# Attention and two dense layers on one core: staging tiles, thresholds on ScalarE, and keys of two heads turned in one go

## The chip, the cores and the metric

One core of a Trainium2 chip runs the kernel. The metric is the device time of one execution in microseconds; lower is better. Engines are named as in the profile: PE is TensorE, DVE is VectorE, ACT is ScalarE, POOL is GpSimd, SP is SyncE, which here only issues DMAs. PEld is the loading of PE's weights, which runs beside its matmuls.

## The reference

There are 4 batches of 8 heads, 576 positions and 64 dimensions a head, all in float32. The attention keeps only scores within tau of the row's maximum; its output is the input of two dense layers with 2048 hidden columns.

```python
scores = scale * np.matmul(q, k.transpose(0, 1, 3, 2))
thresh = np.max(scores, axis=-1, keepdims=True) - tau
scores = np.where(scores >= thresh, scores, -1000000000.0)
scores = scores - np.max(scores, axis=-1, keepdims=True)
attn = np.exp(scores)
attn = attn / (np.sum(attn, axis=-1, keepdims=True) + 1e-09)
x = np.matmul(attn, v)            # then (tokens, heads * dim)
h = x @ w_in;  x = np.where(h >= 1, h, np.where(h <= -1, 0, (h + 1) ** 2 / 4)) @ w_out
h = x @ w_in2; x = (h * np.clip(h + 3, 0, 6) / 6) @ w_out2
```

## The kernel before, in words

Float32 products are made from halves: a number is split into a high part, rounded to PE's fast float32 format (fp32r in the profile), and a low part, the remainder, and the products of the parts are added up in PSUM.

The attention runs over 16 jobs, each a batch and a pair of heads. A job has 9 blocks of 128 query rows: four of each head, and one (block 4) with the last 64 rows of both heads. A block (`em_block`) goes like this: PE makes the scores of 128 rows by 576 keys in a pair of PSUM banks (P0 or P1, in turn); DVE copies them out negated and keeps the row's minimum nm (L329); ACT makes the exponential e with nm as bias (L330); a threshold th = nm + tau is made for each row (L331), on POOL in the first four jobs and on DVE from the fifth on; DVE multiplies e with the mask p <= th and sums the row into z (L334). Three blocks later `em_pt` turns p by PE, and ACT and DVE copy it out of PSUM. In the first five jobs it goes straight into the tile Gf, and the product with the values runs as plain float32. From the sixth job on the copy goes into one of two staging tiles pf (L376, the tail L350 or L352), ACT writes the high part Gh from pf (L379), and POOL the low parts (L380, L381). `pv_chunk` multiplies with the values, a chunk at a time between other work of PE; from the sixth job on its two halves of 64 rows are added by way of a staging tile named fold (L420, L422). After the ninth block `pre_norm` adds 1e-9 to z (L429) and inverts it, and `em_norm` spreads the result over rows by PE, multiplies, and stores the job's output in DRAM.

Queries and keys come in before their job. `load_qk` loads one head's queries (twice side by side, in qn) or keys (kn, one tile for all). `pre_k` splits a head's keys into the tile ksp, on POOL but for the very first (L233, L234). `unit_qk` turns them by 5 transposes into a P bank and copies them out: the queries split by ACT and DVE (L270, L271), the keys as they are by ACT (L280). A job's four such units stand at its blocks 0, 1 and, for the next job, 5 and 6.

The weights of the dense layers arrive as raw 64-bit words and are put together by `split_a` and `split_b` over ACT, DVE and POOL. During the attention `split_a` clears the sign bit on DVE (L119) and clips on POOL (L121); afterwards ACT takes the absolute value (L124).

When the first batch has its four jobs, pieces of the first dense layer (`dense1`, lines L540 to L608) are woven in: after each third of an attention step a credit of 0.3484 is added, and pieces are emitted while it lasts. What is left comes after the attention, and then the rest of both layers (L540, L582).

The order of the text is the order of priority. A planner puts each engine's instructions in order when the kernel is built, by its own model of their durations, and sets the waits; each engine then works through its list in order. DMAs are all issued from SP's list, in order.

Of the kernel before, what the change touches and what calls it, by code (L numbers as in the profile page):

```python
# [18 lines left out]
def kernel(  # L19
# [12 lines left out]
    nc = tc.nc  # L32
# [20 lines left out]
    CSTEP = 2  # L53
    RAW = 3
# [12 lines left out]
    three = const.tile([128, 1], F32, name="three")  # L67

# [39 lines left out]
    def split_a(kind, m, f):  # L108
# [104 lines left out]
    def load_qk(j, nm, h):  # L213
# [3 lines left out]
        src = (q if nm == "q" else k)[b, 2 * hp + h]  # L217
        main = src[0:MAIN, :].rearrange("(p c) d -> p c d", c=4)
        if nm == "q":
            nc.sync.dma_start(out=qn[h][:, 0:4], in_=main.unsqueeze(2).to_broadcast([128, 4, 2, D]))  # L220
            nc.sync.dma_start(out=qn[h][64 * h:64 * h + TAIL, 4],
                              in_=src[MAIN:SEQ, :].unsqueeze(1).to_broadcast([TAIL, 2, D]))
        else:
            nc.sync.dma_start(out=kn[:, 0:4, :], in_=main)
            nc.sync.dma_start(out=kn[0:TAIL, 4, :], in_=src[MAIN:SEQ, :])

    def pre_k(j, h):
# [28 lines left out]
    def unit_qk(j, nm, h):  # L256
# [3 lines left out]
        if nm == "q":  # L260
            n = qn[h].rearrange("p c r d -> p c (r d)")
            for c in range(5):
                x = T.transpose(tm[:, c * 128:(c + 1) * 128], n[:, c, :], ident)
                if c == 0:
                    pe_pins.append(x)
            load_qk(j + 1, "q", h)
            hi, lo = qst[h]
            sc = taus[:, 1:2]
            tm = tm[:, 0:MAIN + 128]
            S.activation(out=hi, in_=tm, func=ACTF.Copy, scale=sc)  # L270
            V.scalar_tensor_tensor(out=lo, in0=tm, scalar=sc, in1=f32(hi), op0=ALU.mult, op1=ALU.subtract)  # L271
        else:
            n = f32(natt.pop(("ks", j, h))).rearrange("p c r d -> p c (r d)")
            for c in range(4):
                x = T.transpose(tm[:, c * 128:(c + 1) * 128], n[:, c, :], ident)
                if c == 0:
                    pe_pins.append(x)
            T.transpose(tm[:, MAIN:MAIN + 128], n[:, 4, :], ident)
            kst[j, h] = ap.tile([128, SEQ], F32R, tag=f"kst{h}", name="kst")
            S.activation(out=kst[j, h], in_=tm[:, 0:SEQ], func=ACTF.Copy)  # L280

# [26 lines left out]
    def em_block(j, i):  # L308
# [20 lines left out]
        V.tensor_scalar(out=p, in0=s, scalar1=-1.0, scalar2=3e38, op0=ALU.mult, op1=ALU.min, accum_out=nm)  # L329
        S.activation(out=e, in_=p, func=ACTF.Exp, bias=nm, scale=-1.0)  # L330
# [549 lines left out]
```

## Time and profile before

| | us |
|---|---|
| median of 3 runs | 1207.64 |
| lowest and highest | 1205.75, 1208.53 |
| the profiled execution, and its span | 1205.04, 1203.3 |
| PE busy | 1151.6 (96%) |
| PEld busy | 990.1 (82%) |
| POOL busy | 717.2 (60%) |
| ACT busy | 707.8 (59%) |
| DVE busy | 672.0 (56%) |

The attention's first score block is copied out at 9.9 us of the span, and its last at 499; the woven dense work starts at some 150 us. Busy shares over the whole span mix these parts with the dense layers, so they are read by stretch. PE's busy time counts the tails of pipelined matmuls.

### The profile page before, as it was taken

To read this page: it belongs to the slowest core of one execution; us is meant where nothing else is said; L and a number is where in the kernel's file an instruction comes from. 1 tells how busy PE (TensorE), PEld (TensorE's weight loads), DVE (VectorE), ACT (ScalarE), POOL (GpSimd) and SP (SyncE) were. 2 spreads that over 40 slices of the span, in tenths; PEclk is the share of its full clock that TensorE was granted. 3 is DMA by queue.
4 is the path that set the end of the run, shared out by engine and by line. 5 is a ranking of instruction groups with operands and counts; after the bars stand their busy time and mean duration, and the time that the engine had idled before them with its cause. 6 is when DMAs were issued, how large, how long until landed. Compare 5 with 4: busy or idle time off the path is not lost.

```text
span 1203.3 us, 19343 instructions
## 1 busy us (share of the span) xinstructions
PE 1151.6 (96%) x6820; PEld 990.1 (82%) x6820; DVE 672.0 (56%) x1433; ACT 707.8 (59%) x1332; POOL 717.2 (60%) x745
## 2 busy tenths in 40 slices
PE   7899999999998998979999999999999999999998
PEld 5666679988887998979888998888888888888886
DVE  6989997888878788765142465565641121121111
ACT  6777788888878788757354676655542222233222
POOL 5888679999988898947252566656742222222221
PEclk9999999999999999989999999999999999999999
DMA  6444431122221220134121244443210010010000
GB/s 162 129 126 129 137 111 45 43 73 56 55 78 52 55 77 22 35 109 129 62 70 36 88 136 141 160 152 113 88 31 27 1 57 10 1 45 1 18 1 36
DMA packets 99857, 87.08 MB, mean 72 GB/s; under 512 B 51376, under 2 KB 83632, under 8 KB 99760
## 3 DMA queue, kind: packets, MB, share of 16 engines
q1 hardware_dynamic: 99760, 85.85, 24.0%
q8 instruction: 54, 0.88, 0.3%
q14 instruction: 43, 0.35, 0.1%
HBM read 68.52 MB, written 17.30 MB: 71 GB/s over the span
## 4 chain that ended last, share of the span: by engine, by line
PE 70%; POOL 12%; DVE 8%; issue 4%; ACT 3%; DMA 2%; SPq 0%; POOLq 0%; DVEq 0%; ACTq 0%
PE Q L540 29%; PE P L582 26%; POOL Gl L380 6%; PE Q L597 4%; PE P L318 3%; PE Q L408 3%; POOL Gh L381 2%; DVE p L334 2%; PE Q L355 2%; PE Q L410 2%; DVE p L329 2%; POOL vst L294 1%; POOL gl L558 1%; POOL ksp L234 1%; DVE xl L524 1%
## 5 line engine op out<-in xcount | busy, mean ns | idle before, releaser
L558 POOL TENSOR_TENSOR gl<-r,gh 128x512 fp32r<-128x512 f32 (+1 forms) x190 | 202.5, 1066 | 374.9 <-ACT gh L557 355.1
L540 PE MATMUL Q<-xh,wih 128*128 128x512 f32 (+1 forms) x760 | 261.9, 345 | 2.4 <-DVE r L551 2.0
L540 PE MATMUL Q<-xl,wih 128*128 128x512 f32 (+1 forms) x760 | 257.7, 339 | 3.2 <-DVE xl L524 3.2
L540 PE MATMUL Q<-xh,wil 128*128 128x512 f32 (+1 forms) x760 | 257.4, 339 | 0.0
L554 DVE SCALAR_TENSOR_TENSOR r<-r,Q 128x512 f32<-128x512 f32 (+1 forms) x80 | 50.6, 634 | 247.2 <-ACT r L553 247.1
L557 ACT ACTIVATE gh<-r 128x512 fp32r<-128x512 f32 (+1 forms) x190 | 99.6, 524 | 120.1 <-PE P L582 50.5
L540 PEld LDWEIGHTS Q<-xh,wih 128*128 128x128 f32 x760 | 144.6, 190 | 20.9 <-DVE r L551 3.2
L540 PEld LDWEIGHTS Q<-xl,wih 128*128 128x128 f32 x760 | 144.8, 191 | 19.8 <-DVE xl L524 3.6
L540 PEld LDWEIGHTS Q<-xh,wil 128*128 128x128 f32 x760 | 144.5, 190 | 15.3
L380 POOL TENSOR_TENSOR Gl<-pf,Gh 128x512 fp32r<-128x512 f32 (+1 forms) x110 | 147.5, 1341 | 15.2 <-ACT Gh L379 9.4
L334 DVE SCALAR_TENSOR_TENSOR p<-p,th,e 128x576 f32<-128x576 f32 x144 | 149.0, 1036 | 12.7 <-ACT e L330 10.3
L553 ACT ACTIVATE r<-Q,three 128x512 f32<-128x512 f32 (+1 forms) x80 | 51.5, 644 | 143.0 <-PE Q L540 139.5
L330 ACT ACTIVATE e<-p,nm 128x576 f32<-128x576 f32 x144 | 110.9, 772 | 33.3 <-DVE p L329 31.8
L551 DVE SCALAR_TENSOR_TENSOR r<-r,Q 128x256 f32<-128x256 f32 (+1 forms) x110 | 54.5, 496 | 121.1 <-ACT r L550 119.8
L329 DVE TENSOR_SCALAR_CACHE_REDUCE p<-P 128x576 f32<-128x576 f32 x144 | 107.5, 748 | 19.3 <-PE P L305 13.3
L318 PE MATMUL P<-kst,qh 128*128 128x288 f32 x320 | 98.5, 324 | 14.6 <-DVE xu L451 4.5
L582 PE MATMUL P<-woh,gh 128*128 128x512 f32 x288 | 111.9, 390 | 0.6 <-DVE ob L635 0.6
L582 PE MATMUL P<-wol,gh 128*128 128x512 f32 x288 | 112.2, 390 | 0.0
L582 PE MATMUL P<-woh,gl 128*128 128x512 f32 x288 | 110.9, 389 | 0.0
L132 POOL TENSOR_TENSOR w_c<-w_c,w_raw 128x512 int32<-128x512 int32 x64 | 86.2, 1347 | 29.0 <-DVE w_c L130 12.8
L318 PE MATMUL P<-kst,ql 128*128 128x288 f32 x320 | 91.3, 301 | 0.3 <-DVE ql L271 0.3
L355 PE MATMUL Q<-ident,p 128*128 128x128 f32 x576 | 89.0, 276 | 1.9 <-ACT pf L376 1.8
(105 smaller groups left out, 2656.8 us busy)
## 6 DMA issues: line engine op xcount, KB each, us to landing
w_raw<-in_moe_w_in_dram SPq DMA_DIRECT2D x32, 512.0 KB, 4.0
w_raw<-in_moe_w_out_dram SPq DMA_DIRECT2D x32, 512.0 KB, 3.8
qn<-in_q_dram SPq DMA_DIRECT2D x32, 256.0 KB, 3.5
xst<-xd SPq DMA_DIRECT2D x28, 256.0 KB, 3.1
kn<-in_k_dram SPq DMA_DIRECT2D x32, 128.0 KB, 2.6
xd<-xu SPq DMA_DIRECT2D x16, 256.0 KB, 2.4
x2d<-ob SPq DMA_DIRECT2D x16, 256.0 KB, 2.7
xst<-x2d SPq DMA_DIRECT2D x16, 256.0 KB, 3.8
```

The costliest lines, as they stand in the source:

```text
L132: x = G.tensor_tensor(out=c.bitcast(I32), in0=c.bitcast(I32), in1=r, op=ALU.add)
L318: mm = T.matmul(s[:, e, 0:HS], l, r[:, e * HS:(e + 1) * HS], start=(x == 0), stop=(x == len(ops) - 1))
L329: V.tensor_scalar(out=p, in0=s, scalar1=-1.0, scalar2=3e38, op0=ALU.mult, op1=ALU.min, accum_out=nm)
L330: S.activation(out=e, in_=p, func=ACTF.Exp, bias=nm, scale=-1.0)
L334: V.scalar_tensor_tensor(out=p, in0=p, scalar=th, in1=e, op0=ALU.is_le, op1=ALU.mult, accum_out=zt[j][:, i:i + 1])
L355: x = T.transpose(tm[:, cc * 128:(cc + 1) * 128], p[:, cc * 128:(cc + 1) * 128], ident)
L380: G.tensor_tensor(out=lo[:, :, d], in0=f[:, 0:4, b], in1=f32(hi[:, 0:4, d]), op=ALU.subtract)
L540: mm = T.matmul(h, l[:, kk * 128:(kk + 1) * 128], r, start=(x == 0), stop=(x == 3 * KD - 1))
L551: vlast = V.scalar_tensor_tensor(out=r, in0=r, scalar=1.0, in1=h, op0=ALU.min, op1=ALU.max)
L557: x = S.activation(out=gh, in_=r, func=ACTF.Copy)
L558: y = G.tensor_tensor(out=gl, in0=r, in1=f32(gh), op=ALU.subtract)
L582: T.matmul(a, l, r, start=(first and x == 0), stop=(last and x == 2))
```

## The change

- A third staging tile pf.
- The threshold th is made by ACT in all jobs, ahead of the exponential; the addition of 1e-9 to z as well.
- During the attention, too, ACT takes the absolute value in the weight split, in place of DVE's masking.
- kn holds both heads' keys of a job, and `load_k` loads both. In the first four jobs they are split and turned as before. From the fifth job on (JP = 4) one unit at block 5 of the job before turns both heads' keys unsplit, in 5 transposes; for each head ACT copies the high part of its 64 rows out of PSUM, and DVE writes the remainder, out of PSUM too, into the other 64 rows. The second head's tile kst has two buffers.
- The two halves of the product with the values are added by way of the output tile xu, with no tile in between.

```diff
+    NPF = 3
+    JP = 4
...
         x = S.activation(out=r, in_=t[:, :, 0], func=ACTF.Copy, scale=2.0 ** -29)
         after(x, pins["S"])
-
+        x = S.activation(out=f32(c), in_=f32(t[:, :, 1]), func=ACTF.Abs)
         if mode["att"]:
-            x = V.tensor_scalar(
-                out=c, in0=t[:, :, 1], scalar1=0x7FFFFFFF, scalar2=None, op0=ALU.bitwise_and)
             G.tensor_scalar(
                 out=f32(c), in0=f32(c), scalar1=122879.9921875, scalar2=2.0 ** -15, op0=ALU.min, op1=ALU.max)
         else:
-            S.activation(out=f32(c), in_=f32(t[:, :, 1]), func=ACTF.Abs)
...
-    kn = ap.tile([128, 5, D], F32, name="kn")
+    kn = ap.tile([128, 5, 2, D], F32, name="kn")
...
-    pfs = [ap.tile([128, 5, 128], F32, name=f"pf{i}") for i in range(2)]
+    pfs = [ap.tile([128, 5, 128], F32, name=f"pf{i}") for i in range(NPF)]
...
+    def load_k(j):
         if j >= NJ:
             return
+        b, hp = jobs[j]
+        for h in range(2):
+            src = k[b, 2 * hp + h]
+            nc.sync.dma_start(out=kn[:, 0:4, h, :], in_=src[0:MAIN, :].rearrange("(p c) d -> p c d", c=4))
+            nc.sync.dma_start(out=kn[0:TAIL, 4, h, :], in_=src[MAIN:SEQ, :])
+
+    def pre_k(j, h):
+
         n = ap.tile([128, 5, 2, D], F32R, tag="ksp", name="ksp", bufs=1)
         E = V if (j, h) == (0, 0) else G
-        E.tensor_scalar(out=n[:, :, 0, :], in0=kn, scalar1=1.0, scalar2=0.0, op0=ALU.mult, op1=ALU.add)
-        E.tensor_tensor(out=n[:, :, 1, :], in0=kn, in1=f32(n[:, :, 0, :]), op=ALU.subtract)
+        E.tensor_scalar(out=n[:, :, 0, :], in0=kn[:, :, h, :], scalar1=1.0, scalar2=0.0, op0=ALU.mult, op1=ALU.add)
+        E.tensor_tensor(out=n[:, :, 1, :], in0=kn[:, :, h, :], in1=f32(n[:, :, 0, :]), op=ALU.subtract)
         natt["ks", j, h] = n
-        load_qk(j + h, "k", 1 - h)
+        if h == 1:
+            load_k(j + 1)
...
+    def unit_k(j, h):
+
+        if j >= NJ:
+            return
+        tm = unit_bank()
+        if h is not None:
+            turn(tm, f32(natt.pop(("ks", j, h))))
+            kst[j, h] = ap.tile([128, SEQ], F32R, tag=f"kst{h}", name="kst", bufs=1 + h)
             S.activation(out=kst[j, h], in_=tm[:, 0:SEQ], func=ACTF.Copy)
+            return
+        turn(tm, kn)
+        load_k(j + 1)
+        for g in range(2):
+            kst[j, g] = ap.tile([128, SEQ], F32R, tag=f"kst{g}", name="kst", bufs=1 + g)
+            r, o = slice(64 * g, 64 * g + 64), slice(64 - 64 * g, 128 - 64 * g)
+            S.activation(out=kst[j, g][r], in_=tm[r, 0:SEQ], func=ACTF.Copy)
+            V.tensor_tensor(out=kst[j, g][o], in0=tm[r, 0:SEQ], in1=f32(kst[j, g][r]), op=ALU.subtract)
...
+        S.activation(out=th, in_=nm, func=ACTF.Identity, bias=taus[:, 0:1])
         S.activation(out=e, in_=p, func=ACTF.Exp, bias=nm, scale=-1.0)
-        (G if j < 4 else V).tensor_scalar(out=th, in0=nm, scalar1=taus[:, 0:1], scalar2=None, op0=ALU.add)
...
-        f = pfs[mode["n"] % 2]
+        f = pfs[mode["n"] % NPF]
...
-                tmp = ap.tile([64, 320], F32, tag="fold", name="fold", bufs=1)[:, 0:n]
-                S.activation(out=tmp, in_=o[64:128], func=ACTF.Copy)
                 for a, b, d in segs:
-                    V.tensor_tensor(out=xu[j][r, d:d + b - a], in0=o[0:64, a:b], in1=tmp[:, a:b], op=ALU.add)
+                    x = xu[j][r, d:d + b - a]
+                    S.activation(out=x, in_=o[64 - 64 * h:128 - 64 * h, a:b], func=ACTF.Copy)
+                    V.tensor_tensor(out=x, in0=o[r, a:b], in1=x, op=ALU.add)
...
-        V.tensor_scalar(out=z, in0=z, scalar1=1e-9, scalar2=None, op0=ALU.add)
+        S.activation(out=z, in_=z, func=ACTF.Identity, bias=eps)
...
-            if i == 0:
-                at(t, unit_qk, j, "k", 1)
+            if i == 0 and j < JP:
+                at(t, unit_k, j, 1)
...
-            if i == 2:
+            if i == 2 and j + 1 < JP:
                 at(t, pre_k, j + 1, 0)
-            if i == 6:
+            if i == 6 and j + 1 < JP:
                 at(t, pre_k, j + 1, 1)
             if i == 5:
-                at(t, unit_qk, j + 1, "k", 0)
+                at(t, unit_k, j + 1, 0 if j + 1 < JP else None)
...
-    load_qk(0, "k", 0)
-    load_qk(0, "q", 0)
+    load_k(0)
+    load_q(0, 0)
```

## Rows read from the trace of the kernel before

**Rows 1.** By stretch: length, busy us of PE, PEld, DVE, ACT, POOL, clock, DMA.
```profile
10.00:40.00 30.00, 27.05 (x150) 18.46 (x149) 27.13 (x56) 23.29 (x47) 21.31 (x26) 1.00 0.57 157
40.00:150.00 110.00, 103.04 (x573) 68.12 (x571) 102.50 (x223) 81.60 (x175) 87.20 (x95) 0.97 0.46 134
150.00:470.00 320.00, 297.03 (x2307) 278.47 (x2305) 265.92 (x712) 260.68 (x492) 284.90 (x332) 0.99 0.23 63
...
560.00:1200.00 640.00, 638.49 (x3138) 541.80 (x3137) 210.30 (x302) 272.66 (x474) 256.02 (x210) 1.00 0.19 61
```

**Rows 2.** Chain of waits, shares by line: 0 to 150 us, then 150 to 510.
```profile
by line: PE Q L408 18.6%; PE P L318 11.1%; DVE p L334 8.6%; PE Q L355 7.2%; issue 6.4%; DVE p L329 5.3%; DVE w_c L130 3.8%; DMA xst<-xd 3.5%; DMA w_raw<-in_moe_w_in_dram 3.4%; DMA w_raw<-in_moe_w_out_dram 3.1%; DVE w_c L128 3.0%; DMA qn<-in
...
by line: POOL Gl L380 19.4%; issue 8.3%; POOL Gh L381 8.2%; PE Q L597 6.2%; PE Q L540 5.8%; PE P L318 5.7%; PE Q L410 5.4%; DVE p L334 3.6%; PE Q L355 3.5%; POOL vst L294 3.2%; DVE p L329 3.1%; POOL gl L558 3.0%; POOL ksp L234 2.6%; DVE xl 
```

**Rows 3.** Groups, 0 to 150 us: line, shape, count | busy us, mean ns | idle before.
```profile
L119 DVE TENSOR_SCALAR w_c<-w_raw 128x512 uint32<-128x512 uint32 x20 | 12.5, 625 | 0.5 <-DMA w_raw<-in_moe_w_in_dram 0.5
...
L331 POOL TENSOR_SCALAR th<-nm,taus 128x1 f32<-128x1 f32 x36 | 19.4, 538 | 7.7 <-DVE p L329 7.6
```

**Rows 4.** Groups of ACT: L742 of 0 to 150 us, the others of 150 to 510.
```profile
L742 ACT ACTIVATE taus<-half 128x1 f32<-128x1 f32 x1 | 0.2, 203 | 0.0
...
L352 ACT ACTIVATE Gf<-Q 64x64 f32<-64x64 f32 x2 | 0.3, 203 | 0.0
...
L124 ACT ACTIVATE w_c<-w_raw 128x512 f32<-128x512 f32 x2 | 1.4, 676 | 0.0
...
L280 ACT ACTIVATE kst<-P 128x576 fp32r<-128x576 f32 x21 | 13.6, 645 | 0.3
...
L330 ACT ACTIVATE e<-p,nm 128x576 f32<-128x576 f32 x100 | 77.2, 772 | 23.0 <-DVE p L329 22.3
```

**Rows 5.** Groups of POOL, 150 to 510 us.
```profile
L234 POOL TENSOR_TENSOR ksp<-kn,ksp 128x320 fp32r<-128x320 f32 x20 | 18.1, 905 | 0.8
...
L233 POOL TENSOR_SCALAR ksp<-kn 128x320 fp32r<-128x320 f32 x20 | 10.2, 512 | 1.2 <-PE P L278 0.2
...
L380 POOL TENSOR_TENSOR Gl<-pf,Gh 128x512 fp32r<-128x512 f32 (+1 forms) x109 | 146.2, 1342 | 15.2 <-ACT Gh L379 9.4 <-DVE ob L608 1.3 <-PE Q L355 1.2
```

**Rows 6.** Timeline, 300 to 304 us: start, length, what; five transposes' weight loads.
```profile
301.80 0.57 PEld L263 LDWEIGHTS P<-ident,qn 128*128 128x128 f32 x5
```

**Rows 7.** Groups of DVE, 150 to 510 us, L422 by its one shape.
```profile
L331 DVE TENSOR_SCALAR th<-nm,taus 128x1 f32<-128x1 f32 x100 | 19.6, 200 | 0.3
...
L429 DVE TENSOR_SCALAR z<-z 128x9 f32<-128x9 f32 x12 | 9.3, 775 | 0.1
...
L422 DVE TENSOR_TENSOR xu<-Q,fold 64x256 f32<-64x256 f32 x31 | 12.7, 411 | 0.7 <-ACT fold L420 0.2
...
L445 DVE TENSOR_TENSOR xu<-xu,P 128x512 f32<-128x512 f32 x11 | 7.4, 676 | 0.4 <-PE P L443 0.4
...
L334 DVE SCALAR_TENSOR_TENSOR p<-p,th,e 128x576 f32<-128x576 f32 x100 | 104.8, 1049 | 9.4 <-ACT e L330 7.3
```

**Rows 8.** Waits, 150 to 510 us: who <- whom: us in total, times, longest.
```profile
DVE pf L350 <- POOL Gh L381: 20.5, 30, 1.7
...
ACT pf L376 <- POOL Gl L380: 13.2, 20, 1.4
...
DVE p L334 <- ACT e L330: 7.3, 18, 0.8
...
DVE xu L422 <- ACT fold L420: 3.3, 2, 3.1
...
PE P L318 <- DVE ql L271: 0.6, 3, 0.3
```

**Rows 9.** Timeline, 0 to 16 us.
```profile
0.73 0.39 SPq L224 DMA_DIRECT2D kn<-in_k_dram  x1
...
1.79 0.68 SPq L220 DMA_DIRECT2D qn<-in_q_dram  x1
...
5.65 1.27 PE L263 MATMUL P<-ident,qn 128*128 128x128 f32 x5
```

More of the change, by code (lines that the diff above doesn't have):

```diff
@@ L67 @@
     three = const.tile([128, 1], F32, name="three")
+    eps = const.tile([128, 1], F32, name="eps")
     xd, x2p, x2d = ([dram.tile([128, KD, n], F32, name=f"{nm}{w}") for w, n in enumerate(WIDE)]
@@ L254, in unit_bank, with turn, unit_q @@
         return pair_bank(f"P{mode['s'] % 2}").rearrange("p e n -> p (e n)")
-    def unit_qk(j, nm, h):
+    def turn(tm, n):
+        n = n.rearrange("p c r d -> p c (r d)")
+        for c in range(5):
+            x = T.transpose(tm[:, c * 128:(c + 1) * 128], n[:, c, :], ident)
+            if c == 0:
+                pe_pins.append(x)
+    def unit_q(j, h):
         if j >= NJ:
@@ L259, in unit_qk @@
         tm = unit_bank()
[L260 to L279, printed above, removed]
-            S.activation(out=kst[j, h], in_=tm[:, 0:SEQ], func=ACTF.Copy)
+        turn(tm, qn[h])
+        load_q(j + 1, h)
+        hi, lo = qst[h]
+        sc = taus[:, 1:2]
+        tm = tm[:, 0:MAIN + 128]
+        S.activation(out=hi, in_=tm, func=ACTF.Copy, scale=sc)
+        V.scalar_tensor_tensor(out=lo, in0=tm, scalar=sc, in1=f32(hi), op0=ALU.mult, op1=ALU.subtract)
+    def unit_k(j, h):
[5 more added lines that the diff above has]
+            kst[j, h] = ap.tile([128, SEQ], F32R, tag=f"kst{h}", name="kst", bufs=1 + h)
+            S.activation(out=kst[j, h], in_=tm[:, 0:SEQ], func=ACTF.Copy)
+            return
[6 more added lines that the diff above has]
+            V.tensor_tensor(out=kst[j, g][o], in0=tm[r, 0:SEQ], in1=f32(kst[j, g][r]), op=ALU.subtract)
     def unit_v(j, h):
@@ L464, in attention @@
         for t, (j, i) in enumerate(order):
-            if i == 0:
-                at(t, unit_qk, j, "k", 1)
+            if i == 0 and j < JP:
+                at(t, unit_k, j, 1)
             if i == 1:
-                at(t, unit_qk, j, "q", 1)
-            if i == 2:
+                at(t, unit_q, j, 1)
+            if i == 2 and j + 1 < JP:
                 at(t, pre_k, j + 1, 0)
-            if i == 6:
+            if i == 6 and j + 1 < JP:
                 at(t, pre_k, j + 1, 1)
             if i == 5:
-                at(t, unit_qk, j + 1, "k", 0)
+                at(t, unit_k, j + 1, 0 if j + 1 < JP else None)
             if i == 6:
-                at(t, unit_qk, j + 1, "q", 0)
+                at(t, unit_q, j + 1, 0)
             if i in AFTER:
@@ L488, in attention @@
             block = [(em_block, order[t])] if t < len(order) else []
-            mid = [x for x in ev if x[0] in (unit_qk, em_norm)]
+            mid = [x for x in ev if x[0] in (unit_q, unit_k, em_norm)]
             pt = [(em_pt, order[t - LP])] if 0 <= t - LP < len(order) else []
-            last = [x for x in ev if x[0] not in (unit_qk, em_norm)]
+            last = [x for x in ev if x[0] not in (unit_q, unit_k, em_norm)]
             mode["t"] += 1
@@ L738 @@
     G.memset(half, 0.5)
-    for i in range(2):
+    for i in range(NPF):
         G.memset(pfs[i][64:128, 4], 0.0)
     G.memset(three, 3.0)
+    G.memset(eps, 1e-9)
     S.activation(out=taus[:, 0:1], in_=half, func=ACTF.Copy)
@@ L746 @@
     V.tensor_tensor(out=taus[:, 0:1], in0=taus[:, 2:3], in1=taus[:, 3:4], op=ALU.max)
-    unit_qk(0, "k", 0)
-    unit_qk(0, "q", 0)
-    load_qk(0, "q", 1)
+    unit_k(0, 0)
+    unit_q(0, 0)
+    load_q(0, 1)
     pre_k(0, 1)
```

15 lines of the change are left out of this document (5 added, 10 removed).

## The prediction, made before the changed kernel was run

> **What bounds the kernel now.** I read the busy time by stretch first, then the chain of waits cut into two stretches, then the groups by line of the engines that the change touches, then the waits. All sums are made against the profiled execution: its span is 1203.3 us, its own time 1205.04, so 1.7 us lie around the span; the median of the runs, 1207.64, is 2.6 above it, and I add these 2.6 at the end.
>
> From 560 us on PE is busy for 638.5 of 640 us [rows 1]. That is the two dense layers; the change doesn't touch them, and nothing is to be gained or lost there but a shift. What matters is the attention part, and it has two stages with different limits. From 40 to 150 us the blocks run beside the splitting of weights, and DVE is the fullest engine but PE: 102.5 of 110 us, 93%, with ACT at 81.6 (74%) and POOL at 87.2 (79%). From 150 to 470 us, where the first dense layer is woven in, POOL has 284.9 of 320 (89%), DVE 265.9 (83%), ACT 260.7 (81%), and PE 297.0 (93%, tails of pipelined matmuls counted) [rows 1]. PE is idle for only 23 us there and for 7 in the stretch before: that is a ceiling on what any relief of the others can bring.
>
> The chain says which of the full engines is waited for. Before 150 us DVE's listed lines have 8.6+5.3+3.8+3.0 = 21% of it. From 150 to 510 us POOL's have 19.4+8.2+3.2+3.0+2.6 = 36%, PE's 6.2+5.8+5.7+5.4+3.5 = 27%, DVE's 3.6+3.1 = 7%, and no line of ACT is among those listed above 2.6% [rows 2]. I use these shares as weights: work taken from an engine counts at the engine's share of the chain, since for the rest of the time the chain runs elsewhere. For ACT I take 10%, from several lines below the listed ones.
>
> **The first stage, to 150 us.** Removed: the masks on DVE, 20 x 625 ns = 12.5 us, and POOL's thresholds of the first four jobs, 36 x 538 ns = 19.4 us [rows 3]. Added on ACT: 20 absolute values at the 676 ns that the same operation takes later, 13.5 us, and a threshold for each block; the nearest rows of a tiny ACT instruction are 203 ns, one of 128x1 and two of 64x64 [rows 4], so 45 x 0.203 = 9.1 us. In the stretch from 40 to 150 (110 of the 140 us from 10 on, so 15.7 of the 20 splits and 36 blocks) that takes DVE to about 102.5 - 15.7 x 0.625 = 92.7 (84%) and lifts ACT to about 81.6 + 15.7 x 0.676 + 36 x 0.203 = 99.5 (90%): ACT becomes the fullest. If the fullest engine can again be filled to 93%, the stretch takes 99.5/0.932 = 106.8 instead of 110, and over the 140 us from 10 on that is 4.1 us. I take -4. The ends: -12.5, if DVE stays what is waited for, and +9, if each threshold simply delays its exponential, which stands behind it on ACT, and with that DVE's masked product, 45 times.
>
> **From the fifth job on.** Keys: POOL loses 24 pairs of 512 + 905 ns [rows 5], 34.0 us; at 36% of the chain -12.4. The ends are 0 (another engine is just as full) and -34. PE turns the keys of a job in 5 transposes instead of 10: 60 fewer, of 0.57/5 = 0.114 us each by the loads of five [rows 6], 6.8 us, at 27% -1.8 (0 to -6.8). On DVE the thresholds go, 108 x 200 ns = 21.6 us, and the addition to z, 12 x 775 ns = 9.3 us; 24 subtractions out of PSUM of 64x576 come, none of which is in the trace. An addition out of PSUM takes 411 ns for 256 elements and 676 for 512 [rows 7], so 1.04 ns an element and 742 ns for 576; 17.8 us. The balance is -13.1 us, at 7% -0.9. As bounds of a subtraction I take 676 and 1049 ns, the smaller addition and the masked product of the same width. ACT gets 108 thresholds, 12 additions and about 11 more copies (the fold of group c is now two pieces), 131 x 0.203 = 26.6 us, at 10% +2.7; the two key copies of a job cost what they did (645 ns each [rows 4]), as the time goes by columns. If ACT is waited for all the time, it is the whole 26.6.
>
> The new key unit holds its PSUM bank longer: copy, subtraction, copy, subtraction, about 0.645 + 0.742 + 0.645 + 0.742 = 2.8 us against 0.57 + 0.645 = 1.2 for each head before. What is queued behind it on PE is the next-but-one block's scores, which need this bank. Its nearest row is the query unit, which holds a bank for a copy and a subtraction of 640 columns: PE waited for that three times, 0.6 us in all [rows 8]. Ends 0 and 12 x 1.6 = +19; near the row, +1.
>
> The third staging tile removes waits of DVE for POOL (20.5 us, 30 times) and of ACT for POOL (13.2 us, 20 times) [rows 8]. But a full POOL releases no earlier because it has one more tile in its queue; the wait moves one tile on. What it can win is POOL's own idle time, 15.2 us ahead of its subtractions, 9.4 of these for ACT [rows 5]. Ends 0 and -15, and -3 for an engine that stays over 80% full. The fold through xu itself takes away the single staging tile; DVE waited 3.3 us for it [rows 8]; with the same order of work I cost it at nothing.
>
> **The start and the SP queue.** Both heads' keys are now loaded before the first query. On SP two more issues stand ahead of it: key to query were 0.73 to 1.79, 1.06 us apart, and the first query transposes began at 5.65, 3.9 after that issue [rows 9]; I take it that they wait for these bytes. So +1.1, hidden by nothing, since nothing else runs yet. In its favour, the second head's keys need no second trip; the block that wants them comes later, so 0. Later key loads stand behind the transposes or the split of the job before, a whole job (some 30 us) ahead of use: 0, and so for the loads behind them on SP.
>
> **Sum.** The planner lays out each engine's order anew at the build, and I can't see that order; I take it as kept. -4 - 12.4 - 1.8 - 0.9 + 2.7 + 1 - 3 + 1.1 = -17.3: 1205.0 - 17.3 = 1187.7, and with the 2.6 to the median 1190.3. I forecast 1190 us, with a range of its own from 1176 to 1202.
>
> **A rule weighed.** The exponential, which has a per-partition bias as the threshold will have, takes 772 ns for 576 columns [rows 4]. The Trainium skill, page "ScalarE: Activation LUTs", section "What ACT_TABLE_LOAD costs", gives 280 ns plus 0.833 ns a column for that form, 760 ns here, so the trace agrees; by it a threshold would cost 280 ns and not 203. The sum by the page's price would be an estimated 1 us later.
>
> **Rivals.**
> *ACT takes POOL's place.* From 150 to 470 us ACT has 260.7 us, and ten jobs add 110 x 0.203 = 22.3: 283, 88.4% of 320, as full as POOL is now. Filled like POOL the stretch takes 283/0.89 = 318 us: nothing won but 2 us, and with the first stage and the start 1205 - 5 + 2.6 = 1203; if the first stage gives nothing either, 1208. For it: every score block and every transposed p passes through ACT. Against it: ACT is on no listed piece of the chain after 150 us. 20%, spread over 1202 to 1211.
> *ACT can't be filled that far: slower.* ACT's exponential and its copies out of PSUM free the banks that PE needs next, while POOL worked from buffered tiles. A threshold at the head of each block's exponential then delays the block. If ACT can be kept only 84% full, the stretch takes 283/0.84 = 337 us, 17 more, 19 over the 360 us of that stage; less 4 and plus 1 elsewhere, and the 2.6: 1224. It decides where ACT can't be filled beyond 88%. For it: DVE already waits 7.3 us for exponentials, 18 times [rows 8]; against it, those are 18 of 100. The Trainium skill's "Rules for kernel authors" on the same page speaks for this rival: additions and maxima belong on VectorE, not ScalarE. No row of before shows a threshold on ACT. 14%.
> *Everything opens up.* If POOL was the cause of most of PE's idle time, the 23 + 7 us and 3 more of the first stretch go [rows 1], with the 6.8 of transposes: 1205 - 40 + 2.6 = 1168. For it: POOL's 36% of the chain, and the lifted waits. Against: part of PE's gaps are the chain through exponential and masked product, which gets longer by the threshold. 10%.
>
> **Chances.** The forecast has 56%. Faster by over 0.2% (below 1205.2; 0.2% is about what a measurement of this kernel can tell from no change): 56 + 10 + 10 of the first rival = 76%. Same: 7%. Slower: 3 + 14 = 17%. The range, 1172 to 1214, reaches down past the forecast's own for the lower ends of keys and staging, and up over the first rival; about 7% lie below and 12% above.
>
> **What would show it.** Thresholds on ACT near 0.2 us, and in the middle stage ACT close to 88% full with POOL near 80%; DVE's wait for POOL at the tail copy far below 20 us; POOL's share of the chain under 25%; the first query transposes a microsecond later; subtractions of keys near 0.74 us; the dense layers unchanged in length. ACT below 85% full with the exponential high on the chain and no shorter stage would make the forecast wrong; so would PE waiting over 10 us for the key unit's bank.

## The result and the profile after

The changed kernel took 1222.59 us (median of 4 runs, 1219.39 to 1225.35) where the kernel before took 1206.70 in the same comparison (1205.29 to 1208.53): a ratio of 1.013, interval [1.0097, 1.0163]. It is slower by 16 us; the forecast was 17 us faster. The profiled execution took 1225.35, its span is 1223.6, 20.3 more than the span before. It is the slowest of the four, and at 0.983 it has the lowest mean clock of them.

Where the 20.3 us lie, from the timelines of both (the start of the 1st, the 37th and the last copy of scores, then the first matmul of 512 columns, with which the dense part begins):

| stretch | before, us | after, us | difference | forecast |
|---|---|---|---|---|
| to the first score copy | 9.85 | 11.10 | +1.3 | +1.1 |
| first four jobs | 107.4 | 115.9 | +8.4 | -4 |
| later twelve jobs | 381.8 | 383.6 | +1.8 | about -14 |
| to the first 512-column matmul | 65.8 | 66.8 | +1.0 | 0 |
| dense part | 638.4 | 646.2 | +7.8 | 0 |

By stretch, after (columns as in [rows 1]):
```profile
40.00:150.00 110.00, 100.38 (x534) 64.21 (x533) 87.54 (x187) 92.62 (x219) 67.38 (x61) 0.95 0.45 126
150.00:470.00 320.00, 295.20 (x2247) 274.36 (x2246) 260.92 (x635) 276.06 (x602) 252.84 (x286) 0.98 0.24 65
470.00:560.00 90.00, 79.38 (x593) 76.46 (x593) 59.62 (x128) 65.87 (x151) 61.56 (x69) 0.92 0.23 68
560.00:1200.00 640.00, 640.00 (x3165) 538.88 (x3165) 214.66 (x309) 277.95 (x487) 261.26 (x215) 1.00 0.20 62
```
The work moved as forecast: from 150 to 470 us POOL fell from 284.9 to 252.8 (79%) and ACT rose from 260.7 to 276.1 (86%); before 150, DVE fell from 102.5 to 87.5 [rows 1]. But PE is no fuller for it, and its clock is lower in each of the first three stretches. For the third, the row of before:
```profile
470.00:560.00 90.00, 81.72 (x648) 79.77 (x647) 63.82 (x138) 66.68 (x144) 64.75 (x70) 0.96 0.25 78
```

The chain of waits after, 150 to 510 us:
```profile
by line: PE P L334 9.3%; PE Q L556 8.0%; POOL Gl L396 8.0%; issue 7.5%; DVE p L350 7.0%; PE Q L426 6.2%; PE Q L613 6.2%; PE Q L371 5.5%; POOL Gh L397 3.7%; ACT e L347 3.6%; DVE p L345 3.5%; PE Q L424 2.7%; POOL vst L310 2.3%; POOL gl L574 2
```
POOL's listed lines fell from 36% [rows 2] to 16%. PE, DVE and ACT took the share over, and the stretch is no shorter. PE's own waits for POOL's low parts, in the same stretch, were short already before:
```profile
PE Q L410 <- POOL Gl L380: 9.5, 11, 1.3
```
and are little shorter after:
```profile
PE Q L426 <- POOL Gl L396: 7.3, 6, 2.8
```

The waits after, 150 to 510 us (columns as in [rows 8]):
```profile
POOL Gl L396 <- ACT Gh L395: 29.4, 20, 4.6
DVE p L345 <- PE P L321: 25.7, 23, 3.6
DVE pf L366 <- POOL Gh L397: 12.1, 17, 1.7
...
DVE p L350 <- ACT e L347: 8.3, 19, 0.9
```
DVE's wait for POOL at the tail copy fell from 20.5 to 12.1 us [rows 8], as expected. In its place POOL now waits 29.4 us for ACT (9.4 before [rows 5]), and DVE 25.7 (13.3 before) for the transposes of an earlier block's last columns (L321), which PE makes in the scores' banks right behind a block's scores. The emptier POOL here waits longer for what feeds it.

The new operations, groups after, 150 to 520 us (columns as in [rows 4]):
```profile
L346 ACT ACTIVATE th<-nm,taus 128x1 f32<-128x1 f32 x101 | 29.2, 289 | 9.2 <-DVE p L345 8.9
...
L296 DVE TENSOR_TENSOR kst<-P,kst 64x576 fp32r<-64x576 f32 x21 | 15.9, 755 | 1.5 <-ACT kst L295 0.9
```
A threshold took 289 ns against the 203 that I used; a key subtraction 755 against 742. But ACT begins the exponential while its threshold is still ending, here 0.18 us after the threshold's start (median 0.185 over the kernel):
```profile
203.24 0.28 ACT L346 ACTIVATE th<-nm,taus 128x1 f32<-128x1 f32 x1
203.42 0.76 ACT L347 ACTIVATE e<-p,nm 128x576 f32<-128x576 f32 x1
```
From 150 to 470 us ACT's busy time would be 10.2 us less without its 90 thresholds, 0.11 us each.

**How PE's time adds up.** The prediction took PE's idle time as the ceiling of any gain and left its clock out. Here is the key unit of the job at 305 us in the kernel after; first the instructions (start, length, what):
```profile
305.34 0.71 PE L264 MATMUL P<-ident,kn 128*128 128x128 f32 x5
...
307.39 0.28 PE L426 MATMUL Q<-Gh,vst 128*128 128x256 f32 x1
307.51 0.28 PE L426 MATMUL Q<-Gl,vst 128*128 128x256 f32 x1
...
308.67 0.66 PE L371 MATMUL Q<-ident,p 128*128 128x128 f32 x4
312.35 1.30 PE L264 MATMUL P<-ident,qn 128*128 128x128 f32 x5 [3.03 <-issue]
...
314.73 0.41 PE L556 MATMUL Q<-xh,wih 128*128 128x256 f32 x1
314.94 0.41 PE L556 MATMUL Q<-xl,wih 128*128 128x256 f32 x1
```
then DVE's order in the same stretch:
```profile
307.32 3.15 DVE L540 TENSOR_TENSOR xl<-xst,xh 128x256 fp32r<-128x256 f32 x4
310.51 0.75 DVE L296 TENSOR_TENSOR kst<-P,kst 64x576 fp32r<-64x576 f32 x1
311.29 0.76 DVE L345 TENSOR_SCALAR_CACHE_REDUCE p<-P 128x576 f32<-128x576 f32 x1
...
313.81 0.76 DVE L296 TENSOR_TENSOR kst<-P,kst 64x576 fp32r<-64x576 f32 x1
```
and the stretches around:
```profile
306.00:311.00 5.00, 3.21 (x26) 2.68 (x24) 4.94 (x10) 4.88 (x11) 3.24 (x4) 1.00 0.26 59
311.00:317.80 6.80, 5.45 (x26) 5.48 (x27) 5.18 (x12) 4.29 (x8) 5.00 (x5) 0.51 0.27 68
317.80:323.00 5.20, 4.57 (x37) 4.31 (x37) 1.72 (x5) 2.69 (x6) 2.47 (x4) 0.98 0.17 60
```
The unit held its PSUM bank from 305.3 to 314.6. DVE was full (4.94 of 5 us), and its order decides: four splits of the dense layer's input stood ahead of the key subtraction, and that ahead of the copy of the block's scores, which were ready from 308.6. The query's transposes, which take the other pair of banks, began 0.3 us after that copy had ended; the profile names no releaser, so that they waited for it is read from the times. PE stood idle for 3.03 us. From 311.2 us on the granted clock stood at its half level (1.2 GHz) for 6.8 us, and matmuls of 256 columns began 0.21 us apart instead of 0.12. A stall of PE can so be paid twice; it isn't always (see the last section).

Up to 560 us the clock records show 17.1 us at the half level before, in four stretches, and 41.0 after, in eight. Priced at half their length, that is (41.0 - 17.1)/2 = 11.9 us. PE's idle gaps up to the first 512-column matmul add up to 46.9 us before and 55.4 after: 8.5 more. The 60 transposes that are gone are worth 6.8. 8.5 + 11.9 - 6.8 = 13.6, and that part of the span grew by 12.5. I use this sum for every run. It is bookkeeping of PE's time: it says where the time went, not why PE idled. The Trainium skill, page "TensorE: Matmul & The Clock Gate", section "HAM oscillation — how this bites in real kernels", prices time at the half level the same way, at half of it; the sum here agrees within 1.1 us. The clock's term is that of the profiled execution. By their mean clocks (0.987, 0.987, 0.988, against 0.992 before) the change's other three runs lost an estimated 5 to 6 us to it.

### The profile page after: what moved, and what is told of

Its sections match the earlier page's. It is cut to its first block, busy times and chain, and to the rows that moved or that the text cites. A ratio compares the mean times of both kernels' runs of the same rounds, so it can differ in the third digit from the quotient of the medians.

```text
span 1223.6 us, 19110 instructions
## 1 busy us (share of the span) xinstructions
PE 1163.4 (95%) x6760; PEld 989.1 (81%) x6760; DVE 649.3 (53%) x1313; ACT 744.4 (61%) x1523; POOL 664.0 (54%) x663
## 4 chain that ended last, share of the span: by engine, by line
PE 73%; DVE 9%; POOL 6%; ACT 5%; issue 3%; DMA 2%; SPq 1%; POOLq 0%; ACTq 0%; DVEq 0%
PE Q L556 29%; PE P L598 26%; PE Q L613 4%; PE P L334 4%; DVE p L350 3%; PE Q L424 3%; POOL Gl L396 2%; PE Q L371 2%; PE Q L426 2%; DVE p L345 2%; ACT e L347 1%; POOL Gh L397 1%; DMA w_raw<-in_moe_w_in_dram 1%; PE P L264 1%; POOL vst L310 1%
## 5 line engine op out<-in xcount | busy, mean ns | idle before, releaser
L574 POOL TENSOR_TENSOR gl<-r,gh 128x512 fp32r<-128x512 f32 (+1 forms) x190 | 205.5, 1082 | 388.8 <-ACT gh L573 370.1
L396 POOL TENSOR_TENSOR Gl<-pf,Gh 128x512 fp32r<-128x512 f32 (+1 forms) x110 | 142.1, 1291 | 40.5 <-ACT Gh L395 30.5
L350 DVE SCALAR_TENSOR_TENSOR p<-p,th,e 128x576 f32<-128x576 f32 x144 | 146.3, 1018 | 23.6 <-ACT e L347 22.9
L334 PE MATMUL P<-kst,qh 128*128 128x288 f32 x320 | 101.3, 331 | 15.1 <-DVE ql L278 5.5
```

The source lines that it names most:

```text
L334: mm = T.matmul(s[:, e, 0:HS], l, r[:, e * HS:(e + 1) * HS], start=(x == 0), stop=(x == len(ops) - 1))
L350: V.scalar_tensor_tensor(out=p, in0=p, scalar=th, in1=e, op0=ALU.is_le, op1=ALU.mult, accum_out=zt[j][:, i:i + 1])
L396: G.tensor_tensor(out=lo[:, :, d], in0=f[:, 0:4, b], in1=f32(hi[:, 0:4, d]), op=ALU.subtract)
L574: y = G.tensor_tensor(out=gl, in0=r, in1=f32(gh), op=ALU.subtract)
```

## The experiments

Ratios are to the kernel before, run on the same chip beside it (medians 1205.8 to 1206.7). In the table, "part" is the profiled time to the first 512-column matmul against before's 564.9; "idle" is PE's idle in it against 46.9, "clock" half of the change in time at the half level (17.1), "dense" the time from there on against 638.4; all in us.

| run | median | ratio, interval | part | idle | clock | dense |
|---|---|---|---|---|---|---|
| the change | 1222.59 | 1.013 [1.0097, 1.0163] | +12.5 | +8.5 | +11.9 | +7.8 |
| e1_pad32 | 1211.57 | 1.0051 [1.0035, 1.0067] | -0.8 | -1.2 | +1.7 | +7.8 |
| e2_pad64 | 1208.00 | 1.0012 [0.9997, 1.0028] | +1.6 | +2.7 | +1.7 | +3.6 |
| e3_nopad | 1216.56 | 1.0085 [1.0058, 1.0111] | +11.3 | +7.5 | +8.5 | 0.0 |
| e4_nopad_th | 1215.58 | 1.0071 [1.0045, 1.0097] | +10.8 | +8.0 | +8.5 | -0.1 |
| e5_th | 1215.32 | 1.007 [1.0044, 1.0096] | +13.1 | +2.2 | +11.9 | -0.4 |
| e6_abs | 1206.63 | 1.0004 [0.9986, 1.0021] | -0.6 | +0.1 | -3.4 | 0.0 |
| e7_keys | 1220.85 | 1.012 [1.0081, 1.0159] | +14.9 | +12.9 | +6.8 | -0.1 |
| e8_pf3 | 1206.15 | 0.9991 [0.9971, 1.0011] | -0.8 | +1.5 | +1.7 | -0.3 |
| e9_bounce | 1218.63 | 1.0093 [1.0065, 1.012] | +13.5 | +12.3 | +8.5 | -0.1 |
| e10_two | 1212.66 | 1.0056 [1.0034, 1.0077] | +8.0 | +3.1 | +8.5 | -0.5 |
| e11_load | 1212.56 | 1.0044 [1.0031, 1.0057] | +8.8 | +5.9 | +3.4 | -0.1 |
| e12_th_late | 1207.00 | 1.0 [0.9985, 1.0015] | +0.5 | -1.3 | +1.7 | -0.4 |
| f1_th_late | 1206.98 | 1.0014 [1.0002, 1.0027] | +3.1 | +2.4 | +6.8 | -0.2 |
| f2_stag | 1220.36 | 1.0132 [1.011, 1.0153] | +12.6 | +6.0 | +13.7 | 0.0 |
| f3_two | 1207.96 | 1.0013 [0.9997, 1.003] | -4.5 | -1.9 | -3.4 | 0.0 |
| f4_gauge | 1207.36 | 1.0005 [0.9987, 1.0024] | -1.7 | +0.1 | -1.7 | 0.0 |
| g1_two | 1208.06 | 1.0014 [0.9998, 1.0031] | +2.9 | -1.3 | +6.8 | 0.0 |
| g2_start | 1214.72 | 1.0069 [1.0044, 1.0093] | +8.8 | +8.2 | +8.5 | -0.1 |

Idle plus clock, less 6.8 where the joint unit takes 60 transposes away (e3, e4, e7, e9, f1, f2, g2), gives the part within 2.2 us for all but e2, e6, e8, e10 and g1 (within 4.0). So the longer times are accounted for, up to these remainders, by PE's work, its idle time and its clock. A single profile carries its own scatter in the clock column; the medians decide which edit costs time.

**e1_pad32: only the place of the tiles.** The change's new constant `eps` takes 32 bytes of each partition, and all tiles allocated behind it from that end (weights, x, the hidden layer) lie 32 bytes further on; those allocated from the other end stay. The edit adds to the kernel before a tile of that size that nothing uses:
```
+    pad = const.tile([128, 8], F32, name="pad")
...
+    G.memset(pad, 0.0)
```


> The kernel before with one unused constant tile of 32 bytes a partition behind the other constants, so that every tile of the weights, and most of the dense layers' tiles, moves up by 32 bytes as the new tile eps moves them in the changed kernel; each engine's order of instructions is that of before but for one memset. Theory A (place): the output matmuls of the dense layers, which took 227 ns before and 232 to 233 after, slow down in the same way, and the run is 6 to 9 us slower than before. Theory B (the dense part's slowness came from the chip or the moment): 227 ns, no difference to before.

It cost 5.2 us of the median, and in the profiled execution the dense part grew by the same 7.8 us as in the change. One stretch of it in four kernels (the count of PE's matmuls is in the first bracket), before:
```profile
920.00:960.00 40.00, 40.00 (x178) 33.15 (x177) 4.82 (x7) 9.25 (x14) 9.03 (x7) 1.00 0.00 1
```
the change:
```profile
920.00:960.00 40.00, 40.00 (x175) 32.52 (x174) 4.12 (x6) 9.68 (x15) 10.37 (x8) 1.00 0.03 10
```
the pad alone:
```profile
920.00:960.00 40.00, 40.00 (x176) 32.53 (x175) 5.08 (x8) 9.42 (x15) 9.30 (x8) 1.00 0.00 1
```
and the change with the tiles back in place (e3):
```profile
920.00:960.00 40.00, 40.00 (x178) 33.14 (x177) 4.83 (x7) 9.88 (x15) 10.66 (x9) 1.00 0.02 7
```
At the full clock in all four, 178 matmuls fit into 40 us with the old place and 175 or 176 with the new one.

**e2_pad64: the same with 64 bytes.**
```
+    pad = const.tile([128, 16], F32, name="pad")
...
```


> The same with a tile of 64 bytes. Theory A1 (what counts is that one operand's address is moved by 32 bytes against the other's within 64): 227 ns and no difference to before. Theory A2 (any shift of the weights against the tiles at the other end of the memory counts): 6 to 9 us slower, as with 32 bytes. Theory B: no difference.

In between: dense +3.6 us, though one more instruction was added here as in e1. Neither A1 nor A2 came out; no simple rule follows from three places.

**e3_nopad: the change without the shift.** `eps` becomes the second column of the tile that holds `three`; every engine's order stays that of the change.
```
+    both = const.tile([128, 2], F32, name="three")
+    three, eps = both[:, 0:1], both[:, 1:2]
```


> The changed kernel with eps as a second column of the constant tile three, so that the weights stand where they stood before; the engines' orders are those of the changed kernel. Theory A: dense part back to 638 us from the first matmul of 512 columns on, and 7 to 9 us faster than the changed kernel: about 1214 us, which leaves the attention's own loss of 7 to 9 us against before. Theory B: as slow as the changed kernel, 1220 to 1224.

6.0 us of the 16 came back and the dense part is 638.4 again. The place is settled both ways. The other 10 us lie in the attention part.

**e4_nopad_th: e3 with all thresholds back** on POOL (first four jobs) and DVE.
```
-        S.activation(out=th, in_=nm, func=ACTF.Identity, bias=taus[:, 0:1])
+        (G if j < 4 else V).tensor_scalar(out=th, in0=nm, scalar1=taus[:, 0:1], ...
```


> The last one, with the thresholds back on POOL (first four jobs) and DVE. Theory T (thresholds of 0.29 us ahead of each exponential on ACT are the attention's loss, the rival on ACT): the attention's end comes back to that of before or earlier, 8 to 15 us faster than with thresholds on ACT, about 1200 to 1207. Theory M (the loss is in the first stage, where the absolute values on ACT delay the weight split): within 4 us of the kernel with thresholds on ACT.

Only 1 us came back: the first four jobs won 6.1 us (114.4 to 108.3), the later ones lost 7.1 (383.1 to 390.2). As one edit it tells nothing; by stages thresholds on ACT look harmful early and helpful late. The next two runs bear out the first and not the second: with them alone, the later jobs are no shorter than before's.

**e5_th: before, with all thresholds on ACT**, the reverse edit.
```
+        S.activation(out=th, in_=nm, func=ACTF.Identity, bias=taus[:, 0:1])
-        (G if j < 4 else V).tensor_scalar(out=th, in0=nm, scalar1=taus[:, 0:1], ...
```


> The kernel before with one part of the change alone: the threshold on ACT ahead of the exponential in all jobs. With thresholds taken back from the changed kernel, its first four jobs were 6 us shorter and its later ones 7 us longer. Theory T (a threshold of 0.29 us ahead of each exponential costs in the first stage, whatever else is changed): the first four jobs take 5 to 8 us more than before's 107.4, and the whole is 1209 to 1216. Theory P (the planner's order of the changed kernel made that loss; the threshold itself costs ACT time that has room): the first four jobs within 3 us of before, the whole within 4 us of 1206.

Slower by 8.9. The first four jobs took 120.3 us instead of 107.4, the later ones 383.0. The stretch from 40 to 150 us:
```profile
40.00:150.00 110.00, 99.25 (x501) 64.80 (x500) 95.76 (x192) 78.98 (x189) 70.66 (x67) 0.88 0.41 117
```
ACT was no fuller than before (79.0 against 81.6 [rows 1]), so a full ACT isn't the reason. The waits from 10 to 150 us are of work held behind other work:
```profile
POOL w_c L132 <- DVE w_c L130: 21.9, 15, 4.4
ACT xu L417 <- PE Q L408: 14.8, 10, 3.1
```
They were 3.8 and 5.6 us before. In the profiled execution the clock, at 0.88 here against 0.97 [rows 1], makes up most of the loss; this execution had the lowest clock of e5's six.

**e12_th_late: before, with thresholds on ACT from the fifth job on.**
```
+        if j < 4:
...
+        else:
+            S.activation(out=th, in_=nm, func=ACTF.Identity, bias=taus[:, 0:1])
```


> The kernel before with thresholds on ACT from the fifth job on only, and on POOL in the first four as before. With thresholds on ACT in all jobs the first four took 120.3 instead of 107.4 us, and the later ones 386.1 instead of 384.5. Theory S (the loss of the thresholds belongs to the first stage): 1205 to 1209. Theory E (a threshold ahead of the exponential delays every block): 1212 or more.

No change (first four jobs 107.3 us, later ones 381.9), so what e5 lost goes with the thresholds of the first four jobs.

**f1_th_late: e3 with the thresholds of the first four jobs back on POOL.**
```
+        if j < 4:
+            S.activation(out=e, in_=p, func=ACTF.Exp, bias=nm, scale=-1.0)
+            G.tensor_scalar(out=th, in0=nm, scalar1=taus[:, 0:1], scalar2=None, op0=ALU.add)
...
```


> The changed kernel with the weights at their old place, and thresholds of the first four jobs back on POOL, the others left on ACT. Theory 1 (thresholds on ACT are what the first stage loses): first four jobs 106 to 110 us instead of 114.5, later jobs as with thresholds on ACT (386), the whole 1208 to 1212. Theory 2 (the joint loads lose it): first four jobs 112 or more, 1214 to 1218.

9.6 us came back, and with e3 15.6 of the 16: along this path of edits the loss goes with the place of tiles and with 36 tiny instructions. But an edit brings a new order of the planner with it: between e3 and f1 PE's list differs in some 1,200 of 6,760 places. In three pairs, each with a new order, the early thresholds on ACT go with longer first four jobs: 120.3 against 107.3 us (e5, e12), 114.4 against 107.2 (e3, f1) and 114.4 against 108.3 (e3, e4, where all thresholds moved). That makes them a likely cause; the runs from f2 on show that an order can do as much.

**e6_abs: before, with the absolute values on ACT alone.**
```
+        x = S.activation(out=f32(c), in_=f32(t[:, :, 1]), func=ACTF.Abs)
-            x = V.tensor_scalar(
-                out=c, in0=t[:, :, 1], scalar1=0x7FFFFFFF, scalar2=None, op0=ALU.bitwise_and)
```


> The kernel before with the absolute values on ACT alone, in place of the masks on DVE. Theory M (DVE was what the first stage waited for, as the prediction had it): the first four jobs take 3 to 8 us less, 1199 to 1203. Theory C (the split of a weight becomes a longer chain over ACT, POOL and DVE, POOL waits for it, as 27.8 us of waits of POOL for DVE in the changed kernel suggest): the first four jobs as long as before or up to 5 us longer, 1206 to 1212.

Nothing: taking 12.5 us of masks off DVE, with as much put on ACT, won no time.

**e8_pf3: before, with the third staging tile alone.**
```
-        f = pfs[mode["n"] % 2]
+        f = pfs[mode["n"] % 3]
...
```


> The kernel before with the third staging tile alone. The prediction gave it 3 us: 1203 to 1204. Theory W (a full POOL only passes the wait on): no difference, 1205 to 1208, with DVE's wait for POOL at the tail copy down from 20.5 us but POOL as full as before.

The wait fell, the time did not. Waits, 150 to 510 us:
```profile
DVE pf L350 <- POOL Gh L381: 8.8, 7, 2.5
```
20.5 us before [rows 8]; POOL's own 284.7 us in the stretch stayed, as the prediction had argued.

**e7_keys: before, with the change's keys alone** (both heads loaded at once; from the fifth job on one joint unit).
```
+        turn(tm, kn)
+        load_k(j + 1)
+        for g in range(2):
...
+            V.tensor_tensor(out=kst[j, g][o], in0=tm[r, 0:SEQ], in1=f32(kst[j, g][r]), op=ALU.subtract)
...
```


> The kernel before with the keys alone: both heads' keys loaded together, and from the fifth job on turned together and split out of PSUM. Theory K+ (POOL's relief by 34 us and 60 transposes less are worth what the prediction said): later jobs 12 to 16 us shorter, 1192 to 1196. Theory K0 (POOL's share of the chain passes to others at once): jobs from the fifth on within 4 us of before's 384.5, and a start 1.3 us later: 1204 to 1209. Theory K- (the PSUM bank held for both heads delays the blocks behind it): later jobs 5 to 15 us longer, 1212 to 1222, with PE waiting for the split of the keys.

The dearest part: +14.4 us, PE idle +12.9 though POOL is down to 246.0 us from 150 to 470. The next three take it apart.

**e9_bounce: e7, with the bank copied out whole by ACT first**, then split from SBUF.
```
+        kf = ap.tile([128, SEQ], F32, tag="kf", name="kf", bufs=1)
+        S.activation(out=kf, in_=tm[:, 0:SEQ], func=ACTF.Copy)
...
```


> The keys alone on the kernel before, but ACT first copies the turned keys of both heads out of PSUM in one go, and the split works from that copy: one more ACT copy of 128x576 a job. With the keys alone, the unit held its PSUM bank for 5.3 to 8.6 us from the first transpose to the last subtraction, and the step from block 6 to 7 grew from 5.8 to 8.3 us in the later jobs. Theory H (the hold of the bank is the loss): the hold falls to 1.5 to 3 us, the step from block 6 to 7 to 6 us or less, and the whole to 1204 to 1211. Theory L (the loss is in the work that moved to DVE and ACT, or in the planner's order): 1216 to 1225.

The hold fell to between 1.4 and 4.0 us, and only 2 us came back, where theory H had 1204 to 1211. DVE got dearer: 282.0 us from 150 to 470 against 266.4 in e7, with 1093 ns for a subtraction from SBUF against 754 out of PSUM. So the hold alone isn't shown to be the loss.

**e10_two: e7 with two units a job**, each turning both heads and splitting one.
```
-        for g in range(2):
+        for g in (h,):
...
```


> The keys alone on the kernel before, but in two units at their old places, each of which turns both heads' keys, as 5 transposes, and splits its one head out of PSUM: as many transposes as before, none of POOL's splitting, half the hold. Theory H: holds of 2 to 3.5 us, the whole 1202 to 1210, POOL's relief included. Theory L: 1216 to 1225, since the same work is on DVE and ACT.

8.2 us came back without the saved transposes, and PE idled 9.8 us less: in this pair one unit that waits twice for DVE was worse than two. The same edit won 12.4 us from f2 to f3 and nothing from f1 to g1 (below), so how much of it is the unit and how much the new order stays open.

**e11_load: e7 with all keys turned head by head**, so that the joint load is all that's left.
```
-    JP = 4
+    JP = 16
```


> The kernel before with both heads' keys loaded together and nothing else of the change: every job's keys are split on POOL and turned as before. The start is 1.3 us later. Theory H: 1206 to 1209. Theory L or one in which the loads and the SP queue make the loss of the keys: 1212 or more.

As slow as e10, and the pair bears on the prediction's largest term. From 150 to 470 us, e10:
```profile
150.00:470.00 320.00, 299.42 (x2300) 280.62 (x2301) 273.10 (x736) 259.24 (x491) 258.01 (x289) 0.98 0.25 66
```
and e11:
```profile
150.00:470.00 320.00, 296.84 (x2286) 276.33 (x2285) 266.96 (x713) 257.55 (x490) 283.96 (x327) 0.99 0.24 64
```
26 us less on POOL, and the medians are 0.1 us apart. PE idled 2.8 us less and lost 5.1 more to its clock. The pair isn't POOL's relief alone: e10 also has the 24 key subtractions on DVE (18 us) and another order. But over all runs, eleven kernels here have the keys off POOL, the change among them, each in an order of its own, and none is faster than before.

**f2_stag: f1 with the first four jobs' keys loaded head by head**, to take back what e11 seemed to charge for the load.
```
+        if j + 1 < JP:
+            load_k(j + 1, (h,))
...
```


> The last one with the keys of the first four jobs loaded head by head as before. Both theories: the start 1.3 us earlier. Theory 2: first four jobs 4 to 6 us shorter than the last kernel's; theory 1: within 2 us of it, the whole 1206 to 1211.

The opposite: 13.4 us slower than f1. So the joint load is no cost that comes off by taking it back, and what e11 lost isn't shown to be the load's.

**g2_start: f1 with one load moved**, the first job's second-head keys behind the first query.
```
-    load_k(0)
+    load_k(0, (0,))
...
+    load_k(0, (1,))
```


> The kernel with thresholds of the first four jobs on POOL (1207.0, joint loads), with one difference: the second head's keys of the very first job are loaded behind the first queries, as before; all later loads stay joint. Theory of loads: the start 1.1 to 1.3 us earlier and nothing else, 1205 to 1207. Theory O (a new order from the planner moves the time by itself): the first four jobs or the later ones differ by 4 us or more in either direction, though no load of theirs is moved.

7.7 us slower, 5.4 of it in the later jobs, where no load moved. What moved with it is the order that the planner laid out: PE's list differs from f1's in some 1,200 of 6,760 places, ACT's in some 430 of 1,487. Here a new order goes with 5 to 8 us. It needn't: in e6, e8 and e12 PE's list differs from before's in some 950 to 1,760 places, and the times are before's.

**f4_gauge: before, with one step planned later**, to measure that directly.
```
-                at(t + 1, pre_norm, j)
+                at(t + 2, pre_norm, j)
```


> The kernel before with the inverse of the row sums taken one step later: same instructions, another order from the planner. It gauges what a new order alone does. Theory G (a new order costs or wins some us by chance): 3 us or more from before in either direction. Theory N (order is worth little): within 2 us of 1206.

The planner changed two places on POOL, so this gives no such measure. In effect it repeats the kernel before: 1207.36, from 1202.91 to 1210.44.

**f3_two: f2 with two key units a job, and g1_two: f1 with two**, both by e10's edit.
```
-        for g in range(2):
+        for g in (h,):
...
```


> The last one with two key units a job from the fifth on, each turning both heads and splitting one. Theory H (the hold of the PSUM bank for 5 to 9 us costs 8 us, as it did with the keys alone): the later jobs shorter by 4 to 9 us than the last kernel's, the whole 1198 to 1205, faster than before. Theory H0 (with thresholds on ACT, DVE has room and the hold costs nothing more): within 2 us of the last kernel.

> The changed kernel with the weights at their old place, thresholds of the first four jobs on POOL, loads of both heads together as in the change, and from the fifth job on two key units a job, each turning both heads' keys and splitting one. On the kernel with loads head by head the two units made the later jobs 12 us shorter. Theory H (half the hold): later jobs 376 to 381 instead of 385, the whole 1198 to 1204, below before. Theory O (what the two units won there was a lucky order): within 3 us of 1207.

Neither beats before. On f2 the two units won 12.4 us, on f1 they won nothing (1208.06 against 1206.98), as theory O has it. f3 as profiled was the shortest of all, a span of 1198.7 at a mean clock of 0.995 (before: 1203.3 at 0.992); its ten runs go up to 1210.84.

**The clock over the runs.** Repeats of one kernel, with the same instructions, differ by up to 10 us, and their time goes with the mean granted clock: over the 245 runs of all kernels, each against its kernel's mean, 0.9 us for 0.001, correlation -0.86. The mean clock was 0.992 in before's runs, 0.983 to 0.988 in the change's and 0.987 in f1's. By that slope f1 would stand an estimated 4.5 us lower at before's clock, about 1202.5. What f1 has to gain by the sum is the 60 transposes (6.8 us), since its PE idles 2.4 us more than before's; the lower clock takes it back. No run held the clock fixed, so this rests on the scatter and on the sums in the table.

## Why the prediction was wrong, step by step

- **"At 36% of the chain -12.4" is the step that failed.** POOL's time fell as forecast and its share of the chain with it, from 36% to 16%, yet PE's idle up to the dense part rose by 8.5 us instead of falling. A share says who is waited for, not what comes free. PE itself waited for POOL's Gl for 9.5 us before and still for 7.3 after, 2.2 us less where the sum had 12.4; waits of ACT and DVE for POOL can stand behind others of PE's waits, but PE's idle time as a whole grew. With DVE at 83% and ACT at 81% [rows 1] other waits took the place. e10 and e11, 26 us of POOL apart, are equally fast, and none of the eleven kernels with the keys off POOL beats before. The end that I gave, 0, is nearest to what they show.
- **PE's clock was no term at all.** I took PE's idle time as the ceiling of a gain and did not ask what more idle would cost, though before's profile had the row (0.97 from 40 to 150 us [rows 1]). In the profiled execution 24 us more at the half level are 11.9 us, its largest single term; in the other three runs it is an estimated 5 to 6.
- **The first stage, -4, came out +8.4.** DVE's relief did come (102.5 to 87.5 us) and won nothing (e6). ACT at 92.6 of 110 was less full than my 99.5. The bound of +9, "if each threshold simply delays its exponential", was near in size; the profile shows such a delay of 0.185 us a threshold. e5, e12 and f1 place the cost with the first four jobs' thresholds. How much of it is the threshold's own place ahead of the exponential and how much the new order is open: g2 and f2 show that an order can move as much.
- **The threshold at 203 ns:** the instruction took 289. The Trainium skill's price ("ScalarE: Activation LUTs", "What ACT_TABLE_LOAD costs": 280 ns plus 0.833 a column) agrees with that length. But ACT overlaps it with the exponential, so that it took 0.11 us of ACT's busy time and delayed the exponential by 0.185. My 203 was near the delay by luck and too much for ACT's time; neither is the cause by itself, since e12 has 108 of these thresholds and lost nothing.
- **The key unit's bank, +1 for a hold of 2.8 us**: it held 5.4 to 9.3, since the four steps wait on two full engines. The nearest row, the query unit, has one step on each. The sign that I gave, "PE waiting over 10 us for the key unit's bank", did not show: the profile puts 0.8 us of PE's waits down to the key subtraction, and the rest, as in the stall at 309 us, is indirect. What the hold costs is open: e9 shortened it and won 2 us, e10 and f3 with two units won 8.2 and 12.4, g1 nothing.
- **The 60 transposes, -1.8:** I took 27% of their 6.8 us. The sums above close with all of it.
- **The third staging tile, -3:** 0 (e8).
- **The planner's order, "I take it as kept":** it wasn't. Between f1 and g2 a new order goes with 7.7 us, more than most terms of the sum.
- **"The dense layers unchanged":** +7.8 us by the 32 bytes of `eps` (e1, e3). Nothing in the profile of before could show it, but the new tile in the diff could have been a rival.
- **Right:** the start, +1.3 for +1.1 (query transposes at 6.57, before 5.65 [rows 9]); the subtraction; POOL at 79% for 80, and ACT at 86% for 88, the latter with thresholds that took less of ACT than I had counted.

The rival "ACT can't be filled that far" named 1224 and a mechanism that is part of it: ACT got to 86%, under its 88. But f1 fills ACT further (280.6 us of 320) and is 15.6 us faster, so ACT's fill wasn't the cause. That its 1224 lies beside the measured 1222.59 is luck: 7.8 us of the change's loss are in the dense part, which that rival left unchanged.

## What to carry to other kernels

Before pricing an edit, see whether it adds a tile, and whether the operands of the long matmuls keep their addresses; test with an unused tile of that size. Where four engines are over 80% full, don't price a relief by its share of the chain: read what PE itself waits for, count what it will idle, and allow for a clock that may fall behind a stall. Where a planner lays out the order anew, a single comparison mixes the edit with a new order, so take edits one by one and from both sides.

## What the runs showed of the hardware

- 32 bytes of address slow the 512-column matmuls: 40.0 us hold 178 of them at one place, 175 or 176 at the other, at the same full clock; the dense part takes 638.4 and 646.2 us. Those of the output layer slowed most (from 227 to 233 ns apart, while the input layer's stayed at 227 to 228). At 64 bytes it was 642.0. Why, no run shows.
- In before and in the change, each fall of the granted clock to its half level came with or after gaps of PE, the longest of them 0.6 to 3 us, and lasted 3.4 or 6.8 us; in other kernels here up to 10.2. A gap of 1.75 us at 390.7 us before was followed by 3.4 us at the half level, the one of 3.03 in the change by 6.8. But not each gap was followed by a fall: those of 2.13 us at 155.6 us before and of 1.68 at 218.8 in the change were not. So these runs give no rule for it.
- An ACT instruction on one column with a per-partition bias takes 289 to 292 ns, against 203 for a column without one [rows 4]. The next instruction on ACT began 0.185 us (median) after its start.
